# Grouped-query attention over a cached K and V: 256 rows of the output weights on four DMA engines, and four smaller edits

## The chip, the cores and the metric

The kernel runs on one core of a Trainium2 chip. The metric is the device time of one launch in microseconds, the median of several runs. Beside the times there is one profiled execution of the kernel, from which all rows below come.

## What is computed

Eight batches of four new tokens attend to 2,048 cached keys. There are 32 query heads and 8 K/V heads, so four query heads share a K/V head. All inputs are bf16.

```python
B, Sq, D = 8, 4, 512
Hq, Hkv, Sk, Dh = 32, 8, 2048, 128
q = (x @ wq).reshape(B, Sq, Hq, Dh).transpose(0, 2, 1, 3)
k = jnp.repeat(k_cache, rep, axis=1)          # rep = 4
v = jnp.repeat(v_cache, rep, axis=1)
scores = jnp.einsum("bhqd,bhkd->bhqk", q, k) * (Dh ** -0.5)
p = softmax(scores)
o = jnp.einsum("bhqk,bhkd->bhqd", p, v)
return o.transpose(0, 2, 1, 3).reshape(B, Sq, Hq * Dh) @ wo
```

K and V are 33.6 MB each, wq and wo 4.2 MB each: 75.5 MB are read once.

## The kernel before

**Units.** The work is cut into 16 units: four K/V heads of one batch each, `units[u] = (hq, b)`. One load of 2 MB brings a unit's K (`load_k`), another its V (`load_v`): 128 partitions, 16 KB contiguous in each. `kpool` and `vpool` hold three of each. All loads are issued by SP on one queue, in the order of the list `loads`: K two units ahead of V, and wo's first quarter between V13 and V14. `load_ready` issues as many as the buffers allow, once per unit; the other three quarters of wo are issued after the loop's unit 15. A load that has to wait holds up what stands behind it on SP. Each load also waits for the one issued eight loads before it, because eight completion semaphores are used in turn.

**One unit.** K arrives with keys in partitions. `transpose_part` (four parts to a unit) turns it on TensorE (PE), two bf16 as one fp32, into `kp` (pool `psum_k`, three banks), and VectorE (DVE) copies it to `kt`. `scores` multiplies with the block-diagonal queries `q_bd` into `s_ps`; ScalarE (ACT) takes EXP and leaves row sums in `l_sb`. `probs_to_keys` turns the result on PE into `pt` (pool `psum_t`, one bank), and ACT copies it in eight pieces to `probs`. `values` is 64 matmuls into `o_ps`, and `finish` writes `oT` and divides by the sums. `norms` makes the divisors in each unit: DVE's `by_gq`, a matmul with ones into `l_ps`, a reciprocal.

**Order.** The engines' orders are written out by hand (`manual_schedule`). Loop step n holds the turns of K of unit n, the scores of unit n - 1, and the values of unit n - 2.

**Output.** After eight units a half of the heads is complete. `to_tokens` turns it so that tokens lie in rows, `to_wo_rows` turns it again into `oP`, whose partitions match the layout of wo: eight rows of wo, 8 KB, in each partition. `project` multiplies with one quarter p of wo, 16 matmuls, accumulating into `out_ps`. The last quarter comes in two loads, six rows and two. After wo, four loads called `spare` of 5, 7, 1 and 3 rows of 64 bytes are issued, whose data nothing reads. ACT then copies `out_ps`, and two DMAs write the output.

Of the kernel before, what the change touches and what calls it, by code (L numbers as in the profile page):

```python
# [14 lines left out]
def kernel(  # L15
# [18 lines left out]
    G = 4  # L34
# [10 lines left out]
    KB, VB = 3, 3  # L45
    scale = float(Dh) ** -0.5
# [3 lines left out]
    assert Dh == 128 and C == 64 and J == 8 and HQ == 16 and NU == 16 and T == 32  # L50

# [6 lines left out]
    psum_k = ctx.enter_context(tc.tile_pool(name="psum_k", bufs=3, space=bass.MemoryType.PSUM))  # L58
# [3 lines left out]
    psum_l = ctx.enter_context(tc.tile_pool(name="psum_l", bufs=1, space=bass.MemoryType.PSUM))  # L62
# [6 lines left out]
    probs = [const.tile([128, C, G, HQ], BF16, name=f"probs{i}") for i in range(2)]  # L69
    ident = const.tile([128, 128], BF16, name="ident")  # L70
    ident4 = const.tile([128, 128], FP32, name="ident4")
    ones = const.tile([128, 128], FP32, name="ones")
    by_hq = const.tile([128, 2, HQ], FP32, name="by_hq")
    oT = [const.tile([128, HP, 2, B, Sq], BF16, name=f"oT{n}") for n in range(2)]
# [3 lines left out]
    spare = const.tile([16, 4, 32], BF16, name="spare")  # L78
# [5 lines left out]

    def load_k(u):
        hq, b = units[u]
        ks[u] = kpool.tile([128, C, Dh], BF16, tag="k_sb", name="k_sb")
        nc.sync.dma_start(
            ks[u][:, :, :],
            k_cache[b, G * hq : G * hq + G].rearrange("g (s c) d -> (g s) c d", c=C),  # L90
        )

    def load_v(u):
        hq, b = units[u]
        vs[u] = vpool.tile([128, C, Dh], BF16, tag="v_sb", name="v_sb")
        rows = v_cache[b, G * hq : G * hq + G].rearrange("g (s c) d -> (g s) c d", c=C)
        nc.sync.dma_start(vs[u][:, :, :], rows)

    def load_wo(p, r0, n):
        rows = wo[p * HP * 128 : (p + 1) * HP * 128, :].rearrange("(q r) j -> q r j", r=WR)  # L100
        nc.sync.dma_start(wo_sb[:, p, r0 : r0 + n, :], rows[:, r0 : r0 + n, :])  # L101

    load_k(0)
# [3 lines left out]
    for u in range(2, NU + 2):  # L107
        if u < NU:
            loads.append(("k", u))
        if u == NU:  # L110
            loads.append(("w", 0))
        loads.append(("v", u - 2))
    loads.reverse()

    def load_ready(nk, nv):

        while loads:
            kind, u = loads[-1]
            if kind == "w":
                load_wo(u, 0, WR)  # L120
            elif u >= (nk + KB if kind == "k" else nv + VB):
                return
            else:
                (load_k if kind == "k" else load_v)(u)
            loads.pop()
# [6 lines left out]
    nc.gpsimd.memset(probs[0][:, :, :, :], 0.0)  # L132
    nc.gpsimd.memset(probs[1][:, :, :, :], 0.0)  # L133
    nc.gpsimd.memset(ones[:, :], 1.0)
    nc.vector.tensor_reduce(
        out=by_hq[:, :, :],
        in_=ident4[:, :].rearrange("p (z c q) -> p z q c", z=2, q=HQ),
        axis=AX,
        op=ADD,
# [4 lines left out]
    def transpose_part(u, t):  # L144

        k4 = ks[u][:, :, :].rearrange("s c d -> s (c d)").bitcast(FP32)
        if t % 2 == 0:
            kt[(u, t // 2)] = ktpool.tile([128, 2 * J, 128, 2], BF16, tag="kt", name="kt")
        for half in range(2):
            j0 = t % 2 * J + half * J // 2  # L150
            kp = psum_k.tile([128, J // 2, 128], FP32, tag="k", name="kp")
            for j in range(J // 2):
                w = (t * J + half * J // 2 + j) * 128
                nc.tensor.transpose(kp[:, j, :], k4[:, w : w + 128], ident4[:, :])  # L154
            nc.vector.tensor_copy(  # L155
                out=kt[(u, t // 2)][:, j0 : j0 + J // 2, :, :].rearrange("k j s e -> k (j s e)"),
                in_=kp[:, :, :].rearrange("k j s -> k (j s)").bitcast(BF16),
            )
# [52 lines left out]
    l_sbs = {}  # L211

    def scores(u):

        hq, b = units[u]
        s_sbs[u] = small.tile([128, J, 2, S, 2], BF16, tag="s_sb", name="s_sb")
        l_sbs[u] = small.tile([128, 2], FP32, tag="l_sb", name="l_sb")
        for y in range(2):
            s_ps = psum_s.tile([128, 2 * J, S], FP32, tag="s", name="s_ps")
            for e in range(2):  # L220
                for m in range(4):
                    g, th = m // 2 * 2 + y, m % 2
                    nc.tensor.matmul(  # L223
                        s_ps[m * 32 : (m + 1) * 32, :, :],
                        lhsT=q_bd[:, hq, e, g, b, :, :],
                        rhs=kt[(u, th)][:, :, g * S : (g + 1) * S, e],
                        start=(e == 0),
                        stop=(e == 1),
                    )
            nc.scalar.activation(  # L230
                out=s_sbs[u][:, :, y, :, :].rearrange("r j s w -> r j w s"),
                in_=s_ps[:, :, :].rearrange("r (j w) s -> r j w s", w=2),
                func=EXP,
                accum_out=l_sbs[u][:, y : y + 1],
            )

    def probs_to_keys(u):
# [7 lines left out]
        pr = probs[u % 2][:, :, :, :].rearrange("s (x i k w) g q -> s x g i k w q", x=2, k=4, w=2)  # L245
        for x in range(2):
            for g in range(G):
                z, y = g // 2, g % 2
                nc.scalar.copy(  # L249
                    out=pr[g * S : (g + 1) * S, x, g, :, :, :, :],  # L250
                    in_=halves[(2 * x + y) * S : (2 * x + y + 1) * S, z, :, :, :, :],
                )

    r_sbs = {}

    def norms(u):
        by_gq = small.tile([128, 2, 2, HQ], FP32, tag="by_gq", name="by_gq")
        nc.vector.tensor_tensor(  # L258
            out=by_gq[:, :, :, :],
            in0=l_sbs[u][:, :].unsqueeze(1).unsqueeze(3).to_broadcast([128, 2, 2, HQ]),  # L260
            in1=by_hq[:, :, :].unsqueeze(2).to_broadcast([128, 2, 2, HQ]),
            op=MULT,
        )
        l_ps = psum_l.tile([128, NQ], FP32, tag="l", name="l_ps")
        nc.tensor.matmul(  # L265
            l_ps[:, :],
            lhsT=ones[:, :],
            rhs=by_gq[:, :, :, :].rearrange("k z y q -> k (z y q)"),
            start=True,
            stop=True,  # L270
        )
        r_sbs[u] = small.tile([128, NQ], FP32, tag="r_sb", name="r_sb")
        nc.vector.reciprocal(r_sbs[u][:, :], l_ps[:, :])  # L273
# [3 lines left out]
    def values(u, half):  # L277
        if half == 0:
            o_pss[u] = psum_o.tile([128, NQ], FP32, tag="o", name="o_ps")
        for i in range(half * C // 2, (half + 1) * C // 2):  # L280
# [4 lines left out]
                rhs=probs[u % 2][:, i, :, :].rearrange("s g q -> s (g q)"),  # L285
# [4 lines left out]
    def finish(u):  # L290
        hq, b = units[u]
        nc.vector.tensor_tensor(  # L292
            out=oT[hq][:, :, :, b, :].rearrange("d h p s -> d p h s"),
            in0=o_pss[u][:, :].rearrange("d (p h s) -> d p h s", p=2, h=HP),
            in1=r_sbs[u][:, :].rearrange("d (p h s) -> d p h s", p=2, h=HP),
            op=MULT,
        )

    def to_tokens(n):
        nat = psum_l.tile([2 * T, HP, 128], BF16, tag="l", name="nat")  # L300
        for h in range(HP):
            nc.tensor.transpose(
                nat[:, h, :], oT[n][:, h, :, :, :].rearrange("d p b s -> d (p b s)"), ident[:, :]
            )
        nc.vector.tensor_copy(out=nat_sb[:, :], in_=nat[:, :, :].rearrange("t h d -> t (h d)"))

    def to_wo_rows(n):
        perm = psum_l.tile([128, WR, 2, T], BF16, tag="l", name="perm")
        by_row = nat_sb[:, :].rearrange("t (q r) -> t r q", r=WR)
        for r in range(WR):  # L310
            nc.tensor.transpose(
                perm[:, r, :, :].rearrange("q p t -> q (p t)"), by_row[:, r, :], ident[: 2 * T, : 2 * T]
            )
        nc.vector.tensor_copy(out=oP[n][:, :, :, :], in_=perm[:, :, :, :])

    def project(p, r0, n):
        for r in range(r0, r0 + n):
            for half in range(2):
                nc.tensor.matmul(  # L319
                    out_ps[half * T : (half + 1) * T, :],  # L320
                    lhsT=oP[p // 2][:, r, p % 2, :],
                    rhs=wo_sb[:, p, r, half * DH : (half + 1) * DH],
                    start=(p == 0 and r == 0),
                    stop=(p == NP - 1 and r == WR - 1),
                )

    for n in range(1, NU + 2):
# [7 lines left out]
        if w >= 0:  # L335
            norms(w)
        if n < NU:
            transpose_part(n, 2)
        if n == NU - 1:
            probs_to_keys(n - 1)  # L340
        if n == NU + 1:
            out_ps = psum_s.tile([2 * T, DH], FP32, tag="s", name="out_ps")
            project(0, 0, WR)
# [16 lines left out]
        if n == NU - 1:  # L360
            assert not loads, loads
            for p, r0, k in [(1, 0, 8), (2, 0, 8), (3, 0, 6), (3, 6, 2)]:
                load_wo(p, r0, k)
            for i, k in enumerate([5, 7, 1, 3]):
                nc.sync.dma_start(spare[:k, i, :], x.flatten_outer_dims()[:k, :32])

    to_tokens(1)
    project(1, 0, WR)
    to_wo_rows(1)
    project(2, 0, WR)  # L370
    for r in range(0, WR, 2):
        project(3, r, 2)
# [34 lines left out]
```

## Time and profile before

| | |
|---|---|
| median of 3 runs | 187.62 us (187.45, 187.62, 190.75) |
| the profiled execution's own time | 187.35 us |
| its span | 185.6 us |
| PE, DVE, ACT busy | 74%, 56%, 55% of the span |
| HBM read | 75.53 MB, 407 GB/s over the span |
| packets of the load queue (q1) | 95.9% of 16 engines' span |
| granted TensorE clock, mean | 0.98 |

The span runs from the first to the last thing that the profiler records; 1.75 us of the execution's time lie around it. In groups of instructions a row reads: line, engine, operation, output<-input, count, then busy microseconds and mean nanoseconds of one, then the engine's idle time before them and what ended it. A queue row gives packets, megabytes and the time that the packets took as a share of the 16 DMA engines' time. A wait row gives microseconds in total, times, and the longest. `q8 instruction` and `q14 instruction` are transfers that bring the engines their own instructions.

### The profile page before, as it was taken

What the parts mean: (1) busy time and instruction counts of PE and PEld (TensorE: products, weight loads), DVE (VectorE), ACT (ScalarE), POOL (GpSimd) and SP (SyncE); (2) the same over time, 40 slices, a digit from 0 to 9 for tenths busy, and PEclk for the clock granted to TensorE, in tenths of its full rate; (3) what the DMA queues carried; (4) which work ended last, traced back from release to release, by engine and by line L of the source; (5) the groups of instructions that cost most, each with busy time, mean ns of one, the idle gap of its engine ahead of it and who ended that gap; (6) DMA issues with size and microseconds to landing.
All of it is one profiled execution on the core that took longest, in us unless ns stands there. A gap on an engine that the chain in (4) does not pass through costs nothing.

```text
span 185.6 us, 4659 instructions
## 1 busy us (share of the span) xinstructions
PE 137.2 (74%) x2036; PEld 113.4 (61%) x2036; DVE 103.6 (56%) x189; ACT 102.2 (55%) x200; POOL 8.2 (4%) x11
## 2 busy tenths in 40 slices
PE   0092869797978777777777869579777777795872
PEld 0192347595866665757575849377666757585651
DVE  4074188777765747475665756466747475661220
ACT  2000153969576666574839292927566574878700
POOL 8900000000000000000000000000000000000000
PEclk9999589999999999999999999999999999999999
DMA  6998999999999999999999999999999999999970
GB/s 187 484 438 378 434 424 431 434 420 431 438 422 431 422 438 410 441 431 424 434 427 431 434 417 431 441 413 438 424 434 434 417 443 420 417 443 411 417 297 8
DMA packets 5668, 75.86 MB, mean 409 GB/s; under 512 B 688, under 2 KB 784, under 8 KB 1040
## 3 DMA queue, kind: packets, MB, share of 16 engines
q1 hardware_dynamic: 5600, 75.55, 95.9%
q8 instruction: 16, 0.26, 0.5%
q14 instruction: 4, 0.03, 0.0%
q10 hardware_dynamic: 48, 0.02, 0.0%
HBM read 75.53 MB, written 0.03 MB: 407 GB/s over the span
## 4 chain that ended last, share of the span: by engine, by line
DMA 68%; PE 22%; DVE 4%; issue 1%; ACT 1%; SPq 1%
DMA k_sb<-in_k_cache_dram 46%; DMA wo_sb<-in_wo_dram 13%; PE kp L154 12%; DMA x_sb<-in_x_dram 9%; DVE kt L155 3%; PE s_ps L223 3%; PE o_ps L282 3%; PE psq L177 2%; PE l_ps L265 1%; ACT q_bd L202 1%; PE out_ps L319 1%; SPq L101 0%; PE pt L242 0%; DVE by_gq L258 0%; DVE q_bd L202 0%
## 5 line engine op out<-in xcount | busy, mean ns | idle before, releaser
L155 DVE COPY kt<-kp 128x1024 bf16<-128x1024 bf16 x128 | 82.0, 683 | 42.7 <-PE kp L154 42.7
L249 ACT COPY probs<-pt 32x512 bf16<-32x512 bf16 x128 | 73.7, 576 | 49.5 <-PE pt L242 46.7
L154 PE MATMUL kp<-ident,k_sb 128*128 128x128 f32 x512 | 70.6, 284 | 20.2 <-DMA k_sb<-in_k_cache_dram 11.2
L154 PEld LDWEIGHTS kp<-ident,k_sb 128*128 128x128 f32 x512 | 58.3, 147 | 28.8 <-DVE oT L292 9.7
L282 PE MATMUL o_ps<-probs,v_sb 128*128 128x64 bf16 x1024 | 34.8, 194 | 0.2 <-DMA v_sb<-in_v_cache_dram 0.2
L282 PEld LDWEIGHTS <-v_sb 128*128 128x128 bf16 x1024 | 33.9, 98 | 0.8 <-DMA v_sb<-in_v_cache_dram 0.5
L230 ACT ACTIVATE s_sb<-s_ps 128x512 bf16<-128x512 f32 x32 | 22.6, 734 | 1.3 <-PE s_ps L223 0.9
L265 PE MATMUL l_ps<-by_gq,ones 128*128 128x64 f32 x32 | 6.9, 298 | 15.6 <-DVE by_gq L258 15.6
L223 PE MATMUL s_ps<-kt,q_bd 128*32 128x512 bf16 x256 | 17.5, 390 | 0.0
L265 PEld LDWEIGHTS l_ps<-by_gq,ones 128*128 128x128 f32 x32 | 4.8, 188 | 19.5 <-DVE by_gq L258 17.7
L273 DVE RECIPROCAL r_sb<-l_ps 128x64 f32<-128x64 f32 x16 | 8.9, 558 | 9.1 <-PE l_ps L265 9.1
L186 ACT ACTIVATE q_nat<-psq 128x512 bf16<-128x512 f32 x2 | 1.2, 597 | 20.4 <-PE psq L177 20.4
L242 PE MATMUL pt<-ident,s_sb 128*128 128x128 f32 x64 | 9.7, 274 | 2.1 <-ACT s_sb L230 2.1
L292 DVE TENSOR_TENSOR oT<-o_ps,r_sb 128x64 bf16<-128x64 f32 x16 | 3.6, 225 | 13.6 <-PE o_ps L282 13.5
L223 PEld LDWEIGHTS <-q_bd 128*32 128x32 bf16 x256 | 5.6, 94 | 6.1 <-issue 2.5
L242 PEld LDWEIGHTS pt<-ident,s_sb 128*128 128x128 f32 x64 | 7.4, 141 | 2.3 <-ACT s_sb L230 2.3
L230 ACT ACTIVATION_READ_ACCUMULATOR s_sb<-s_ps 128x1 f32 x32 | 6.0, 188 | 0.0
L319 PE MATMUL out_ps<-wo_sb,oP 128*32 128x256 bf16 x64 | 4.2, 273 | 1.1 <-DMA wo_sb<-in_wo_dram 0.6
L374 ACT CAST out_sb<-out_ps 64x256 bf16<-64x256 f32 x1 | 0.4, 365 | 6.9 <-PE out_ps L319 6.9
L319 PEld LDWEIGHTS <-oP 128*32 128x32 bf16 x64 | 3.0, 96 | 1.7 <-issue 0.7
L177 PE MATMUL psq<-wq_sb,xT_sb 128*32 128x512 bf16 x32 | 3.6, 631 | 0.3 <-DVE xT_sb L170 0.3
L133 POOL MEMSET probs<- 128x4096 bf16 x1 | 3.5, 3512 | 0.0
(27 smaller groups left out, 29.9 us busy)
## 6 DMA issues: line engine op xcount, KB each, us to landing
k_sb<-in_k_cache_dram SPq DMA_DIRECT2D x16, 2048.0 KB, 21.6
v_sb<-in_v_cache_dram SPq DMA_DIRECT2D x16, 2048.0 KB, 25.1
wq_sb<-in_wq_dram SPq DMA_DIRECT2D x1, 4096.0 KB
wo_sb<-in_wo_dram SPq DMA_DIRECT2D x3, 1024.0 KB, 20.9
wo_sb<-in_wo_dram SPq DMA_DIRECT2D x1, 768.0 KB, 23.2
wo_sb<-in_wo_dram SPq DMA_DIRECT2D x1, 256.0 KB, 23.4
x_sb<-in_x_dram SPq DMA_DIRECT2D x1, 32.0 KB
spare<-in_x_dram SPq DMA_DIRECT2D x1, 0.3 KB
```

The source lines that it names most:

```text
L154: nc.tensor.transpose(kp[:, j, :], k4[:, w : w + 128], ident4[:, :])
L155: nc.vector.tensor_copy(out=kt[(u, t // 2)][:, j0 : j0 + J // 2, :, :].rearrange("k j s e -> k (j s e)"), in_=kp[:, :, :].rearrange("k j s ...
L177: nc.tensor.matmul(psq[g * T : (g + 1) * T, :], lhsT=xT_sb[:, r, :], rhs=wq_sb[:, r, c0 : c0 + rep * Dh], start=(r == 0), stop=(r == R - 1),)
L223: nc.tensor.matmul(s_ps[m * 32 : (m + 1) * 32, :, :], lhsT=q_bd[:, hq, e, g, b, :, :], rhs=kt[(u, th)][:, :, g * S : (g + 1) * S, e], star ...
L230: nc.scalar.activation(out=s_sbs[u][:, :, y, :, :].rearrange("r j s w -> r j w s"), in_=s_ps[:, :, :].rearrange("r (j w) s -> r j w s", w= ...
L242: nc.tensor.transpose(pt[:, i, :], s4[:, i * 128 : (i + 1) * 128], ident4[:, :])
L249: nc.scalar.copy(out=pr[g * S : (g + 1) * S, x, g, :, :, :, :], in_=halves[(2 * x + y) * S : (2 * x + y + 1) * S, z, :, :, :, :],)
L265: nc.tensor.matmul(l_ps[:, :], lhsT=ones[:, :], rhs=by_gq[:, :, :, :].rearrange("k z y q -> k (z y q)"), start=True, stop=True,)
L273: nc.vector.reciprocal(r_sbs[u][:, :], l_ps[:, :])
L282: nc.tensor.matmul(o_pss[u][:, :], lhsT=vs[u][:, 2 * (th * 2 * J + 2 * (2 * j + x) + w) + c, :], rhs=probs[u % 2][:, i, :, :].rearrange("s ...
L292: nc.vector.tensor_tensor(out=oT[hq][:, :, :, b, :].rearrange("d h p s -> d p h s"), in0=o_pss[u][:, :].rearrange("d (p h s) -> d p h s", ...
L319: nc.tensor.matmul(out_ps[half * T : (half + 1) * T, :], lhsT=oP[p // 2][:, r, p % 2, :], rhs=wo_sb[:, p, r, half * DH : (half + 1) * DH], ...
```

## The change

- **wo.** The first 128 rows of each of wo's first two quarters (256 rows, 256 KB) go to a tile `wo_e` of their own, in partitions 0 to 15 and 32 to 47, by eight loads (`load_wo_e`) of four partitions with 8 KB each. They are issued after V2 to V9, one each. Their counterpart of the attention output is `oE`. In the first two quarters of `wo_sb` a partition then holds seven rows instead of eight.
- **Order of loads.** All of the rest of wo is issued after V15, in ten loads (`WO_PARTS`). K15 and V15 are loaded in two halves. The `spare` loads are gone.
- **Sums.** `norms` is gone. `finish` only copies; `to_tokens` makes all the divisors of a half at once (`by_tok` on GpSimd, two matmuls into `l_ps`, one reciprocal) and divides while it copies `nat` out, with tokens in rows. `oT` and `nat` are fp32.
- **K turns.** `kp` covers two banks, in two buffers, and DVE copies 2,048 bf16 values a time instead of 1,024.
- **Probabilities.** Two of the eight copies of a unit go to DVE (four in the last unit), and `probs` is four tiles of half a unit. `l_ps` and `perm` are taken from `psum_t`, `nat` from `psum_k`.
- The last unit but one turns its probabilities before the third part of K's turns. The projection stands behind the loop.

```diff
+    WO_PARTS = [(p, r, n) for p in (0, 1) for r, n in ((0, 4), (4, 3))]
+    WO_PARTS += [(2, 0, 4), (2, 4, 4)] + [(3, r, 2) for r in range(0, WR, 2)]
+    NE, WM = 48, 7
...
-    psum_k = ctx.enter_context(tc.tile_pool(name="psum_k", bufs=3, space=bass.MemoryType.PSUM))
+    psum_k = ctx.enter_context(tc.tile_pool(name="psum_k", bufs=2, space=bass.MemoryType.PSUM))
...
+    def load_kv(to, cache, u, parts=1):
+        hq, b = units[u]
+        rows = cache[b, G * hq : G * hq + G].rearrange("g (s c) d -> (g s) c d", c=C)
+        for i in range(parts):
+            cs = slice(i * C // parts, (i + 1) * C // parts)
+            nc.sync.dma_start(to[:, cs, :], rows[:, cs, :])
...
+        load_kv(ks[u], k_cache, u, 2 if u == NU - 1 else 1)
...
+    def load_wo_e(i):
+        p0, k0 = i // 4 * 32 + i % 4, i // 4 * HP * 128
+        rows = wo[k0 : k0 + 16 * WR, :].rearrange("(q r) j -> q r j", r=WR)
+        nc.sync.dma_start(wo_e[p0 : p0 + 13 : 4, :, :], rows[i % 4 : i % 4 + 13 : 4, :, :])
+
     def load_wo(p, r0, n):
-        rows = wo[p * HP * 128 : (p + 1) * HP * 128, :].rearrange("(q r) j -> q r j", r=WR)
+        w, k0 = (WM, p * HP * 128 + 16 * WR) if p < 2 else (WR, p * HP * 128)
+        rows = wo[k0 : (p + 1) * HP * 128, :].rearrange("(q r) j -> q r j", r=w)
         nc.sync.dma_start(wo_sb[:, p, r0 : r0 + n, :], rows[:, r0 : r0 + n, :])
 
+    nc.gpsimd.memset(wo_e[:, :, :], 0.0)
     load_k(0)
...
-        if u == NU:
-            loads.append(("w", 0))
         loads.append(("v", u - 2))
+        if 4 <= u < 12:
+            loads.append(("e", u - 4))
...
-        for half in range(2):
-            ...
+        kp = psum_k.tile([128, J, 128], FP32, tag="k", name="kp")
+        for j in range(J):
+            w = (t * J + j) * 128
+            nc.tensor.transpose(kp[:, j, :], k4[:, w : w + 128], ident4[:, :])
+        nc.vector.tensor_copy(
...
+                on_dve = x == 1 if u == NU - 1 else g == 0
+                (nc.vector.tensor_copy if on_dve else nc.scalar.copy)(
...
-    def norms(u):
...
     def to_tokens(n):
+        by_tok = small.tile([128, 2, 2, B, Sq], FP32, tag="by_tok", name="by_tok")
+        for y in range(2):
+            nc.gpsimd.tensor_tensor(
+                out=by_tok[:, y, :, :, :],
...
+        l_ps = psum_t.tile([2 * T, 2, rep], FP32, tag="t", name="l_ps")
...
+        nc.vector.reciprocal(r_sb[:, :], l_ps[:, :, :].rearrange("t y h -> t (y h)"))
+        nat = psum_k.tile([2 * T, HP, 128], FP32, tag="k", name="nat")
+        for h0 in range(0, HP, 4):
...
+            nc.vector.tensor_tensor(
+                out=nat_sb[:, h0 * 128 : (h0 + 4) * 128].rearrange("t (h d) -> t h d", h=4),
+                in0=nat[:, h0 : h0 + 4, :],
+                in1=r_sb[:, h0 : h0 + 4].unsqueeze(2).to_broadcast([2 * T, 4, 128]),
+                op=MULT,
+            )
...
-            for p, r0, k in [(1, 0, 8), (2, 0, 8), (3, 0, 6), (3, 6, 2)]:
+            for p, r0, k in WO_PARTS:
                 load_wo(p, r0, k)
-            for i, k in enumerate([5, 7, 1, 3]):
-                nc.sync.dma_start(spare[:k, i, :], x.flatten_outer_dims()[:k, :32])
...
+    out_ps = psum_s.tile([2 * T, DH], FP32, tag="s", name="out_ps")
     to_tokens(1)
-    project(1, 0, WR)
-    to_wo_rows(1)
-    project(2, 0, WR)
-    for r in range(0, WR, 2):
-        project(3, r, 2)
+    for r in range(WR):
+        project(wo_e[:, r], oE[:, r, :], first=r == 0)
+    for p in range(NP):
+        if p == 2:
+            to_wo_rows(1)
+        for r in range(WM if p < 2 else WR):
+            project(wo_sb[:, p, r], oP[p // 2][:, r, p % 2, :], last=p == NP - 1 and r == WR - 1)
```

## The prediction

> **What bounds the kernel now.** I read the page's slices and queue rows first, then the chain that ended last, SP's waits, and last the tail in half-microsecond windows.
>
> ```profile
> DMA  6998999999999999999999999999999999999970
> ...
> q1 hardware_dynamic: 5600, 75.55, 95.9%
> q8 instruction: 16, 0.26, 0.5%
> q14 instruction: 4, 0.03, 0.0%
> ...
> DMA 68%; PE 22%; DVE 4%; issue 1%; ACT 1%; SPq 1%
> ...
> k_sb<-in_k_cache_dram SPq DMA_DIRECT2D x16, 2048.0 KB, 21.6
> ```
>
> From the second slice to the 38th the 16 DMA engines are as good as full. 75.55 MB pass, and neither kernel moves fewer. The chain is transfers for 68% of the span. A K load lands 21.6 us after its issue, though its own packets take 8 x 0.607 = 4.86 us on each engine: 16.7 us of other work is queued ahead of it.
>
> ```profile
> SPq L88 <- PE kp L154: 94.6, 13, 8.2
> ...
> SPq L365 <- DMA v_sb<-in_v_cache_dram: 12.6, 3, 4.6
> ```
>
> SP issues a K load when PE has turned the old one. Its long waits cost nothing while that queue is full, and PE waits for K too:
>
> ```profile
> PE kp L154 <- DMA k_sb<-in_k_cache_dram: 11.2, 11, 1.9
> ```
>
> So compute has slack in every unit. What can move the end is how the queue drains. In these windows the last two columns are the share of 16 engines busy and GB/s:
>
> ```profile
> 177.50:178.00 0.50, 0.50 (x12) 0.33 (x8) 0.37 (x1) 0.00 (x0) 0.00 (x0) 1.00 1.01 414
> 178.00:178.50 0.50, 0.50 (x11) 0.44 (x8) 0.00 (x0) 0.00 (x0) 0.00 (x0) 1.00 0.78 316
> ...
> 179.50:180.00 0.50, 0.50 (x14) 0.46 (x10) 0.00 (x0) 0.00 (x0) 0.00 (x0) 1.00 0.61 230
> ...
> 180.50:181.00 0.50, 0.11 (x3) 0.11 (x4) 0.00 (x0) 0.00 (x0) 0.00 (x0) 1.00 0.30 115
> 181.00:181.50 0.50, 0.50 (x12) 0.50 (x10) 0.00 (x0) 0.00 (x0) 0.00 (x0) 1.00 0.02 8
> ```
>
> The engines do not stop together: from 178 to 181.2 us fewer and fewer work. The first is done at 177.84, the last at 181.18.
>
> **Why they differ.** No view prints single packets, but the trace holds their start, length and size, and they can be followed: a 16 KB packet is followed on its engine by the next 607 ns later, and each load gives each engine eight packets and a 4-byte completion. Followed so, all 16 engines carry the same 4.72 MB. An engine falls behind by 1.42 us when a 16 KB instruction packet (q8) passes through it, by 0.55 to 0.88 us at an 8 KB one (q14), and by up to 1.1 us at the start. The q8 packets come after every 256 or so PE instructions and go round eight engines; seven of these had two each and end at 180.49 to 181.18, the eighth had one in time and ends at 179.75. The ACT stream's two q14 packets (60.6 and 150.9 us, 63 and 191 ACT instructions in) hit one engine, which ends at 179.50; the two I take for DVE's (52.2 and 159.4 us) another, which ends at 179.87. The other six end at 177.84 to 178.76.
>
> Which engines get the new four-row loads can be read from the old `spare` loads of 5, 7, 1 and 3 rows. Their 64-byte packets stand at the ends of seven engines, in numbers 4, 3, 3, 2, 2, 1, 1: the sets are nested. These engines end at 178.11 (4); 178.45 and 179.50 (3); 177.87 and 179.87 (2); 180.49 and 180.68 (1). A four-row load goes to the first three and one of the two with 2. All are engines without q8 packets, but the three include ACT's. [...]
>
> **The change on the queue.** Packet intervals in the trace: 8 KB 0.305 us, 6 KB 0.230, 2 KB 0.080, completion 0.006. 4 and 3 KB packets are not there; between the 2 and 6 KB rows they are 0.155 and 0.117.
> - wo before, per engine: 24 x 0.305 + 8 x 0.230 + 8 x 0.080 + 5 x 0.006 = 9.83 us.
> - wo after on all 16: 16 x 0.155 + 16 x 0.117 (p = 0, 1), 16 x 0.155 (p = 2), 32 x 0.080 (p = 3), ten completions: 9.45 us.
> - K15 and V15 in halves: 32 x 0.305 for 16 x 0.607, two completions more: +0.06.
> - So every engine saves 0.32 us, and the four pay 8 x (0.305 + 0.006) = 2.49 for `wo_e`: net +2.17.
>
> Counted in the two built programs, PE has 4,090 instructions for 4,096, so q8 stays. ACT has 203 for 238, still past 191: its second packet moves to unit 15's EXP near 168 us, before the end. DVE has 174 for 215: its second packet goes. With the old start offsets:
> - the seven with q8: latest 181.18 - 0.32 = 180.86;
> - the clean ones of the four: at most 178.45 + 2.17 = 180.62;
> - ACT's: 179.50 + 2.17 = **181.67**;
> - DVE's, if it is the fourth: 179.87 - 0.84 + 2.17 = 181.20.
>
> The last byte moves from 181.18 to 181.67: **+0.49 us**. Bounds: 180.86 (-0.32), if ACT's second packet or start offset falls away, and 182.04 (+0.86), if DVE's is among the four and keeps both packets.
>
> [...]
>
> **The tail.** A landing reached PE 0.35 us after the slowest engine's last packet (`wo_sb` part 3a: 180.54, PE at 180.89).
>
> ```profile
> 180.89 1.05 PE L319 MATMUL out_ps<-wo_sb,oP 128*32 128x256 bf16 x16 [0.56 <-DMA wo_sb<-in_wo_dram]
> ...
> 181.97 0.36 ACT L374 CAST out_sb<-out_ps 64x256 bf16<-64x256 f32 x1 [6.92 <-PE out_ps L319]
> ```
>
> The last part was visible at 181.53, while these 16 ran, so the cast came 0.79 us after the last byte. After the change four matmuls wait for the last byte: 0.35 + 0.273 + 3 x 0.052 + 0.03 = 0.81. No gain (+0.02).
>
> **What is hidden, and by what.**
> - PE behind V15: its second half reaches PE near 172.6 (181.67 less 9.45 us of wo, and 0.35). Then 32 values 1.03, `finish` 0.35, eight fp32 turns 1.06, 44 `project` matmuls 2.9, `to_wo_rows` 1.2, p = 2 1.05, twelve of p = 3 0.8: 8.4 us, done near 181.0, while the last byte reaches PE at 182.0. Cover 1.0 us; what is beyond falls on the end. The sums (POOL's two small operations after EXP near 169, two matmuls) run ahead of the turns: 3 us of cover.
> - In the loop DVE loses 128 x 0.683 and 16 x (0.22 + 0.558), and gains 64 x 1.29 (two old copies end to end took that; between 0.68 and 1.37) and 34 probability copies at 0.43 to 0.69 (nearest: 64x1024 `nat_sb` 0.68, 128x512 `oP` 0.43; I take ACT's 0.576): -99.9 + 102.2, about level. PE loses the 15.6 us it waited for `by_gq`. Hidden behind the K waits.
> - `l_ps` and `perm` now share `psum_t` with `pt`: in units 8 and 9 PE stands behind ACT's six copies, 3.5 us each time, and the next K turns stand behind PE. Against 16.7 us queued: nothing.
> - SP issues eleven more DMAs at 0.3 to 0.45 us. An added load waits for the DMA eight before it, a transfer older than the one K waits for. Behind it stand K and V loads; same cover.
> - POOL clears `wo_e` ahead of the identities: 3.5 us (`probs`, 128x4096), identities at 5.2; K0 lets PE start at 8.8. Without that cover PE starts late, yet x lands only at 18.1.
>
> **Sum.** The profiled execution took 187.35 with a span of 185.6; the median is 187.62 and the lower two runs 187.45 and 187.62, so I add to 187.5: 187.5 + 0.49 + 0.02 = **188.0 us**.
>
> **Rivals.**
> 1. *The balance works* (187.2): ACT's engine starts early or loses a packet, and the q8 engines decide at 180.86. For: start offsets differ by up to 1.1 us, and nothing says they repeat. Against: ACT still passes instruction 191. 0.29.
> 2. *The fourth engine is DVE's, with both packets* (188.4): 182.04. Against: 174 instructions. 0.12.
> 3. *The four-row loads do not spread* but sit on one engine: 32 packets x 0.311 = 9.95, so 178.11 - 0.32 + 9.95 = 187.74, 6.6 us late: 194. For: the one-row load did so. Against: the nested spares. It passes 2% from 23 packets on one engine (3.4 us of lead and 3.75). 0.03.
> 4. *`psum_t` starves the queue*: it needs more than 16.7 us of delay at units 8 and 9 and costs what is beyond, so 21 us would make it 192. For: two new waits on one bank. Against: 3.5 us each. 0.02.
> 5. *Over 2% faster* needs 3.75 us, but the mean engine ends at 179.65, so perfect levelling gives 1.5. 0.02.
>
> The forecast has 0.52. The range takes in the bounds, -0.32 and +0.86, and some 0.4 us of run scatter and start offsets on each side: 186.8 to 188.9. Two per cent (3.75 us) is about what a measurement of this kernel can tell from no change; faster, same, slower: 0.02, 0.93, 0.05.
>
> **What would show it.** Right: the drain is shorter but ends later, at 181.4 to 182; K and V loads still land 20 us after issue; three q14 packets instead of four, sixteen q8; the last matmul group is four and waits for `wo_sb`; no `l_ps` rows in the loop. Wrong: gaps in the DMA row before 170 us, a last group waiting for DVE or ACT, or a queue end below 181.

## Result, and the profile after

The changed kernel takes 204.8 us (median of 4 runs, 204.07 to 206.99) against 187.7 us for the kernel before on the same chip: a ratio of 1.094 [1.083, 1.104]. The forecast was 188.0, in a range that ended at 188.9. The profiled execution took 204.72 us with a span of 202.9 (before: 187.35 and 185.6). Some executions of a kernel come out 1.5% or more above its fastest (before: 190.75 for 187.45 us), and the ratios leave these out, so that medians and ratios need not rank alike.

Of the page of the changed kernel, the slices (5.07 us each), the queue rows and the chain:

```profile
PEclk9999769999999999999999975785699999699769
DMA  6999999999999999999999999999999999991000
GB/s 213 446 452 400 423 436 429 423 433 429 423 439 420 431 425 433 423 436 426 429 426 436 426 426 442 420 426 439 426 352 446 365 354 323 409 382 71 3 3 6
...
q1 hardware_dynamic: 6640, 75.55, 89.1%
q8 instruction: 16, 0.26, 0.5%
q14 instruction: 4, 0.03, 0.0%
...
DMA 33%; PE 31%; ACT 19%; DVE 11%; issue 3%; SPq 0%; ACTq 0%; DVEq 0%
```

Three things differ from before. The transfers end three slices before the program does, so something else sets the end: their share of the chain has gone from 68% to 33%, and ACT and DVE, 1% and 4% before, now hold 30%. The clock row, all nines in the second half before, has a hole from slice 24 to 29 (117 to 147 us) and others near the end. And the moved bytes thin out from slice 30 on (147 us): the queue, never short of work before, is now fed late (SP's longest wait for PE's K turns, 8.2 us before, is 14.7). The packet kinds are as before; there are still four q14 packets.

PE's waits show new rows (the last line here is SP's):

```profile
PE l_ps L309 <- ACT probs L270: 5.0, 1, 5.0
PE perm L338 <- ACT probs L270: 4.9, 1, 4.9
...
PE o_ps L282 <- DVE oT L292: 3.9, 1, 3.9
...
SPq L99 <- PE kp L176: 77.2, 13, 14.7
```

The first two are the two uses of `psum_t` for which the prediction had 3.5 us each "against 16.7 us queued: nothing". The timeline shows the first of them (start, duration, work, and in brackets the wait before):

```profile
115.13 1.23 DVE L177 COPY kt<-kp 128x2048 bf16<-128x2048 bf16 x1 [1.33 <-PE kp L176]
...
116.27 1.37 DVE L270 COPY probs<-pt 32x512 bf16<-32x512 bf16 x2
...
117.75 3.58 ACT L270 COPY probs<-pt 32x512 bf16<-32x512 bf16 x6 [4.94 <-DVE probs L270]
...
121.42 0.56 PE L309 MATMUL l_ps<-by_h,by_tok 128*64 128x4 f32 x4 [4.97 <-ACT probs L270]
```

`pt` is complete at 115.5. DVE takes its two copies out of it first, but stands behind a `kt` copy until 116.27; ACT takes its six only then, until 121.33. For all that time `pt` holds the only buffer of `psum_t`, and PE, which would have gone on with the next unit's K, stands at `l_ps`. In windows around this wait (busy time of PE, weight loads, DVE, ACT, POOL; then granted clock, DMA share, GB/s):

```profile
113.00:117.00 4.00, 3.38 (x76) 3.25 (x76) 2.65 (x4) 0.00 (x0) 0.00 (x0) 1.00 1.01 430
117.00:121.00 4.00, 0.00 (x0) 0.00 (x0) 0.86 (x2) 3.13 (x6) 0.00 (x0) 0.72 0.99 422
121.00:125.00 4.00, 2.80 (x14) 2.18 (x15) 1.03 (x3) 0.33 (x1) 0.00 (x0) 0.50 1.03 442
125.00:129.00 4.00, 4.00 (x28) 2.29 (x27) 1.76 (x2) 1.38 (x3) 0.00 (x0) 0.50 0.99 422
```

The transfers go on at full rate in all four rows. But the clock falls to 0.50 and stays there for 7.6 us after PE has work again (121.4 to 129.0). Eight K turns that took 1.07 us before the wait, at 114.02, take 1.92 behind it, at 124.61. So one wait of 5 us costs PE more than 5 us. When PE begins to turn each unit's K shows the sum (us from the start of the span; "step" is the time from one unit to the next):

| unit | 10 | 11 | 12 | 13 | 14 | 15 |
|---|---|---|---|---|---|---|
| before | 107.3 | 118.4 | 128.1 | 137.8 | 147.5 | 157.2 |
| after | 108.3 | 124.6 | 140.5 | 150.1 | 158.1 | 165.8 |
| after is late by | 1.0 | 6.2 | 12.4 | 12.3 | 10.6 | 8.6 |
| step after | | 16.3 | 15.9 | 9.6 | 8.0 | 7.7 |

Before, the queue sets a step of 9.7 us. PE without hindrance needs some 7.7, so it wins back 2 us a unit. Three units are left after the second wait, and K15 starts 8.6 us late.

The rest is lost behind it. From the start of K15 to ACT's copy of `out_ps` before takes 24.7 us (157.2 to 181.97), after 34.2 (165.8 to 200.08). The tail of the changed kernel:

```profile
185.28 0.57 ACT L270 COPY probs<-pt 32x512 bf16<-32x512 bf16 x1 [0.76 <-DVE probs L270]
185.89 0.70 DVE L270 COPY probs<-pt 32x512 bf16<-32x512 bf16 x1 [0.64 <-ACT probs L270]
...
186.99 3.57 PE L282 MATMUL o_ps<-probs,v_sb 128*128 128x64 bf16 x64 [3.87 <-DVE oT L292]
...
193.81 3.17 PE L355 MATMUL out_ps<-wo_sb,oP 128*32 128x256 bf16 x28
...
200.08 0.37 ACT L406 CAST out_sb<-out_ps 64x256 bf16<-64x256 f32 x1 [14.22 <-PE out_ps L355]
```

PE has nothing to do until the last unit's eight copies are made by ACT and DVE in turn, and until DVE, behind its share of them, has copied unit 14's result to `oT`, which is the wait that ends last. Then it runs at half clock in two stretches (187.0 to 190.4 and 193.8 to 197.3): 64 `values` matmuls in 3.57 us, which took 2.03 for unit 14, and 28 projections in 3.17. Before, the first quarter of the projection stood in exactly this gap.

### The profile page after: what moved, and what is told of

It reads as the page before. It is cut to its first block, busy times and chain, and to the rows that moved or that the text cites. A ratio compares the mean times of both kernels' runs of the same rounds, so it can differ in the third digit from the quotient of the medians.

```text
span 202.9 us, 4597 instructions
## 1 busy us (share of the span) xinstructions
PE 146.6 (72%) x2031; PEld 118.7 (58%) x2031; DVE 112.9 (56%) x134; ACT 83.0 (41%) x166; POOL 13.0 (6%) x18
## 4 chain that ended last, share of the span: by engine, by line
DMA 33%; PE 31%; ACT 19%; DVE 11%; issue 3%; SPq 0%; ACTq 0%; DVEq 0%
DMA v_sb<-in_v_cache_dram 25%; ACT probs L270 14%; PE kp L176 11%; DMA x_sb<-in_x_dram 8%; PE o_ps L282 8%; DVE probs L270 5%; DVE kt L177 4%; ACT s_sb L250 4%; PE out_ps L355 3%; PE s_ps L243 3%; PE pt L262 2%; PE nat L321 2%; PE psq L199 2%; PE perm L338 1%; DVE nat_sb L326 1%
## 5 line engine op out<-in xcount | busy, mean ns | idle before, releaser
L177 DVE COPY kt<-kp 128x2048 bf16<-128x2048 bf16 x64 | 76.9, 1222 | 47.0 <-PE kp L176 46.7
L176 PE MATMUL kp<-ident,k_sb 128*128 128x128 f32 x512 | 72.6, 295 | 19.2 <-DMA k_sb<-in_k_cache_dram 15.9
L270 ACT COPY probs<-pt 32x512 bf16<-32x512 bf16 x94 | 54.2, 577 | 65.6 <-DVE probs L270 57.8
L176 PEld LDWEIGHTS kp<-ident,k_sb 128*128 128x128 f32 x512 | 61.5, 152 | 28.5 <-issue 10.1
L282 PE MATMUL o_ps<-probs,v_sb 128*128 128x64 bf16 x1024 | 37.2, 198 | 10.7 <-DMA v_sb<-in_v_cache_dram 4.7
L270 DVE COPY probs<-pt 32x512 bf16<-32x512 bf16 x34 | 23.1, 679 | 8.2 <-ACT probs L270 5.4
L243 PE MATMUL s_ps<-kt,q_bd 128*32 128x512 bf16 x256 | 20.1, 431 | 0.1
L151 POOL MEMSET probs<- 128x2048 bf16 x4 | 7.0, 1805 | 0.0
L292 DVE COPY oT<-o_ps 128x64 f32<-128x64 f32 x16 | 3.6, 224 | 4.2 <-PE o_ps L282 3.8
L338 PE MATMUL perm<-ident,nat_sb 64*128 64x64 bf16 (+1 forms) x23 | 1.8, 236 | 5.7 <-ACT probs L270 4.9
```

The lines of the kernel that those rows point to most:

```text
L151: nc.gpsimd.memset(probs[i][:, :, :, :], 0.0)
L177: nc.vector.tensor_copy(out=kt[(u, t // 2)][:, t % 2 * J : (t % 2 + 1) * J, :, :].rearrange("k j s e -> k (j s e)"), in_=kp[:, :, :].rearr ...
L243: nc.tensor.matmul(s_ps[m * 32 : (m + 1) * 32, :, :], lhsT=q_bd[:, hq, e, g, b, :, :], rhs=kt[(u, th)][:, :, g * S : (g + 1) * S, e], star ...
L270: (nc.vector.tensor_copy if on_dve else nc.scalar.copy)(out=pr[g * S : (g + 1) * S, g, :, :, :, :], in_=halves[(2 * x + y) * S : (2 * x + ...
L282: nc.tensor.matmul(o_pss[u][:, :], lhsT=vs[u][:, 2 * (th * 2 * J + 2 * (2 * j + x) + w) + c, :], rhs=probs[u % 2 * 2 + x][:, i % 32, :, :] ...
L338: nc.tensor.transpose(perm[: by_row.shape[2], r, :, :].rearrange("q p t -> q (p t)"), by_row[:, r, :], ident[: 2 * T, : 2 * T],)
```

## The experiments

Kernels of one section ran on one chip with the kernel before, whose medians were 187.63, 189.13 and 187.94 us in the three. The changed kernel itself ("after") was measured on another chip. Line numbers differ a little between kernels.

**1. One suspect at a time.** Theory A: the shared bank makes most of the 17 us. Theory B: the split of the copies over ACT and DVE, with its alternation, does. Four kernels: each undone alone, both undone, and the bank shared in the kernel before.

```diff
# e1: bank of their own
-        l_ps = psum_t.tile([2 * T, 2, rep], FP32, tag="t", name="l_ps")
+        l_ps = psum_k.tile([2 * T, 2, rep], FP32, tag="k", name="l_ps")
-            perm = psum_t.tile([128, WR, 2, T], BF16, tag="t", name="perm")
+            perm = psum_k.tile([128, WR, 2, T], BF16, tag="k", name="perm")
# e2: ACT makes all copies
-                on_dve = x == 1 if u == NU - 1 else g == 0
+                on_dve = False
# e3: both of these
# e4: the kernel BEFORE, with
-        nat = psum_l.tile([2 * T, HP, 128], BF16, tag="l", name="nat")
+        nat = psum_t.tile([2 * T, HP, 128], BF16, tag="t", name="nat")
-        perm = psum_l.tile([128, WR, 2, T], BF16, tag="l", name="perm")
+        perm = psum_t.tile([128, WR, 2, T], BF16, tag="t", name="perm")
```

> The changed kernel (204.8 us) with l_ps and perm taken from psum_k instead of psum_t. Theory A (the end is late because PE stands behind the copies of pt in units 8 and 9, 5.0 + 4.9 us, with the clock at 0.5 after each, and because the tail behind K15 is longer by itself): the two waits go, K15's turns start near 158 instead of 165.8, but the tail keeps the serial copies of unit 15 on two engines, so 194 to 198 us. Rival B (only the shared bank costs): 187 to 189. Rival C (the queue ran dry and the bank does not matter): 203 to 205.

> The changed kernel with all copies of pt on ACT, l_ps and perm still in psum_t. Theory A: the waits of l_ps and perm shrink by about 1 us each only, so most of the lag stays, and the last unit's values no longer wait for finish behind DVE's copies (3 us): 198 to 202 us. Rival D (passing the bank between DVE and ACT is what costs, in the loop and at the end): below 193.

> The changed kernel with both edits: l_ps and perm from psum_k, all copies of pt on ACT. Theory A: the lag and the serial copies go, 188 to 191 us. The forecast on record for the queue alone says 188.0. If something else costs (two-bank turns of K, sums on tokens), it stays above 192.

> The kernel before with nat and perm taken from psum_t instead of psum_l, nothing else. Theory A: PE waits 3.5 to 5 us for ACT's copies after units 8 and 9, the clock halves, and as a step can be made up by only some 1.1 us a unit (8.6 against 9.7), 3 to 9 us remain at the end: 191 to 197. Rival (the queue of 16.7 us hides it, as the prediction on record said): 187 to 188.5.

| | split copies | ACT alone |
|---|---|---|
| shared bank | 204.8 (after) | 195.92, ratio 1.044 [1.034, 1.054] (e2) |
| own bank | 196.21, ratio 1.042 [1.034, 1.050] (e1) | 193.07, ratio 1.025 [1.016, 1.034] (e3) |

e1 falls where A had it, e2 below what was expected (198 to 202). Neither theory alone is right. In these medians the two cost more together than singly: the bank 2.9 us where ACT copies alone, 8.6 with the split; the split 3.1 and 8.9. But the intervals of e2 and e3 overlap, and K15 starts 5.9 us later in e2 than in e3 (161.8 for 155.9), so 2.9 is not safe as the price of the bank: e4 below and e10 in part 3 give 5.8 and 5.7. What the traces show is that the split lengthens the time for which the bank is held, and so the waits (4.0 and 4.0 us in e2, 5.0 and 4.9 after) and the stretches at half clock behind them (6.8 and 6.8 us in e2, 10.2 and 10.2 after). Both undone still leave 5.4 us over the kernel before, more than A and B had (the expectation was 188 to 191). So there was a third cause.

e4 came out at 193.41, ratio 1.035 [1.026, 1.044]: the same bank, shared in the kernel before, costs 5.8 us by itself. Its waits, and the window after the first:

```profile
PE perm L311 <- ACT probs L249: 4.0, 1, 4.0
PE nat L302 <- ACT probs L249: 4.0, 1, 4.0
```

```profile
121.00:125.00 4.00, 4.00 (x30) 2.12 (x28) 1.90 (x4) 1.57 (x4) 0.00 (x0) 0.61 1.03 442
```

In the kernel before the clock is 1.00 in this window. Eight K turns take 1.71 us behind e4's wait, and the 16 `scores` matmuls after them 1.90; before, both took 1.06. K15 starts at 163.3 for 157.2, yet the last byte of the queue comes at 181.18, to the hundredth where it came before. The queue did not starve; PE came late, and there was too little time left to make it up.

**2. The tail.** In e3 K15 starts on time (155.9) and the last byte comes at 181.62, but the copy of `out_ps` only at 188.96: 33.1 us from K15 on, nearly the 34.2 of after. Its gap and its windows:

```profile
175.03 2.54 PE L282 MATMUL o_ps<-probs,v_sb 128*128 128x64 bf16 x64 [2.46 <-ACT probs L270]
...
175.00:180.00 5.00, 4.19 (x73) 3.56 (x73) 1.11 (x3) 0.58 (x1) 0.00 (x0) 0.63 0.91 359
180.00:185.00 5.00, 5.00 (x44) 3.12 (x45) 0.68 (x1) 0.00 (x0) 0.00 (x0) 0.50 0.11 41
```

From 180 to 185 us PE is full and at half clock. Two theories: PE idles 2.46 us for the copies, work is missing from that gap, and what follows has to be made up (idle time); or the clock, lowered by that gap, is the cost. e5 fills the gap with projections that are ready, as the kernel before did; e6 moves unit 14's turns back as well; e8 fills it with 16 turns of the identity that nothing reads, so PE does more, nothing is earlier, and only the clock can gain. e7 is the kernel before with the 256 rows on four engines, alone.

```diff
# e5: e3, and ahead of the last unit's values (these projections are then not made behind the loop)
+        if n == NU + 1:
+            out_ps = psum_s.tile([2 * T, DH], FP32, tag="s", name="out_ps")
+            for r in range(WR):
+                project(wo_e[:, r], oE[:, r, :], first=r == 0)
+            for r in range(WM):
+                project(wo_sb[:, 0, r], oP[0][:, r, 0, :])
# e6: e5, and
-        if n == NU - 1:
-            probs_to_keys(n - 1)
         if n < NU:
             transpose_part(n, 2)
+        if n == NU - 1:
+            probs_to_keys(n - 1)
# e8: e3, and ahead of the last unit's values
+        if n == NU + 1:
+            kp = psum_k.tile([128, J, 128], FP32, tag="k", name="kp")
+            for j in range(2 * J):
+                nc.tensor.transpose(kp[:, j % J, :], ident4[:, :], ident4[:, :])
# e7: the kernel BEFORE, with load_wo_e, oE, wo_e and WM = 7 as in the change
```

> e3 (193.1 us) with the projections of wo_e and of p = 0 moved ahead of the last unit's values, where PE waits 2.5 us for ACT's copies, as the kernel before had its first quarter there. Theory A (the rest of the loss is PE's idle wait and the half clock that follows it over the tail): PE loses some 1.6 us of work after the wait and the clock holds: 188.5 to 190. Rival E (the queue's end, 181.6 in e3, already sets the time): 192 to 193.5.

> e5 with probs_to_keys of unit 14 behind the third part of K15's turns again, as in the kernel before. Theory A: PE no longer stands 2.5 us before EXP of unit 14 and the clock does not fall at 160 to 165, so unit 15 comes some 2 us earlier; with the queue then deciding, 187.5 to 188.5 (the forecast for the queue alone was 188.0). Rival: no change against e5.

> The kernel before with the 256 rows of wo on four engines and nothing else of the change (wo's first two quarters with seven rows a partition, eight small loads, wo_e and oE). Queue sum: all engines save 0.6 us, the four pay 2.5: ACT's engine ends at 179.50 + 1.88 = 181.4 for 181.18, so 187.7 to 188.2. [...] Rival (the levelling works): 187.0 to 187.3.

> e3 with 16 throwaway turns of the identity on PE while it waits for ACT's copies of the last unit; all other work where it was. Theory A's part on the clock: the 44 projections and the turns behind them run at the full clock, 189 to 190.5 for 193.1. If only the idle time itself counts and not the clock, nothing is gained: 192.5 to 193.5.

- e5: 188.33, ratio 1.001 [0.997, 1.005], a little better than expected. No difference from the kernel before.
- e8: 189.58, ratio 1.004 [0.999, 1.008], as expected. Its filled gap and its windows:

```profile
170.94 1.95 PE L380 MATMUL kp<-ident 128*128 128x128 f32 x16
173.56 2.03 PE L282 MATMUL o_ps<-probs,v_sb 128*128 128x64 bf16 x64 [0.67 <-ACT probs L270]
...
175.00:180.00 5.00, 4.22 (x70) 3.25 (x68) 1.79 (x4) 0.00 (x0) 0.00 (x0) 1.00 0.92 364
180.00:185.00 5.00, 3.08 (x50) 2.33 (x46) 0.42 (x1) 0.36 (x1) 0.00 (x0) 1.00 0.12 44
```

Work that does nothing, put into the gap, keeps the clock at 1.00, and the copy of `out_ps` comes at 183.64 for 188.96. Not all of this is due to the filling. The profiled execution of e8 lacks a stretch at half clock that e3 and e5 have near 162 to 166 us, and so its unit 14 starts `values` 1.5 us earlier (169.07 for 170.55 and 170.54), ahead of the gap. From the end of unit 14's `values` to the copy e3 takes 16.4 us, e8 12.5 and e5 11.2. So the clock is worth 3.8 us, the larger part, and the work that is missing from the gap another 1.3. The medians of e8 and e5 differ by as much, but their intervals overlap.

- e6: 190.79, of four runs between 188.19 and 193.2, without an interval: inconclusive; no gain is seen. In its profiled execution the half clock near 162 us is gone, as expected, and unit 14's `values` start at 169.09; but e8's start at 169.07 without this edit, and another stretch, from 175.6 to 179.0, takes the gain back.
- e7: 189.08, ratio 0.998 [0.993, 1.003]. The 256 rows on four engines make no difference that can be measured, and the interval is too wide to confirm or exclude the 0.5 us that the sum put on them.

**3. Back on the mended tail, and a better version.** e9 and e10 put the split and the shared bank back into e5, one each. e11 reorders ACT's copies so that those which the first `values` need come first, with only `wo_e`'s projections in the gap; e12 is e11 with the 256 rows in two loads of 16 partitions. That these go over all 16 engines is an estimate from the `spare` loads, whose 7 rows stood on seven engines.

```diff
# e9: e5, and
-                on_dve = False
+                on_dve = x == 1 if u == NU - 1 else g == 0
# e10: e5, with l_ps and perm from psum_t again
# e11: e5, and
-        for g in range(G):
-            for x in range(2):
+        for x in range(2):
+            for g in range(G):
...
-            for r in range(WM):
-                project(wo_sb[:, 0, r], oP[0][:, r, 0, :])
# e12: e11, and
-        p0, k0 = i // 4 * 32 + i % 4, i // 4 * HP * 128
-        nc.sync.dma_start(wo_e[p0 : p0 + 13 : 4, :, :], rows[i % 4 : i % 4 + 13 : 4, :, :])
+        p0, k0 = i // 4 * 32, i // 4 * HP * 128
+        if i % 4 == 0:
+            nc.sync.dma_start(wo_e[p0 : p0 + 16, :, :], rows)
```

> e5 (188.3 us) with the copies of pt split over DVE and ACT again as in the change (two of eight on DVE, alternating four and four in the last unit). Theory A: in the loop the longer bank time (5.8 for 5.0 us) hides behind the wait for K; in the last unit the copies take 5.3 for 4.8 us in turns, and finish of unit 14 stands behind them on DVE, so the last values start 1 to 2 us later: 189 to 190.5. Rival (the split costs only together with the shared bank): 188.0 to 188.6.

> e5 with l_ps and perm in psum_t again. Theory A: PE waits 4 us twice, the clock halves twice, and some 6 us of lag remain at K15's turns (161.8 in e2 against 155.9), which all reach the end: 191 to 194. Rival (with the tail mended the lag is made up): 188 to 189.5.

> e5 with the copies of pt in the order of the kernel before (all of x = 0 first) and only wo_e projected ahead of the last values. The last values can start after four copies instead of seven and no longer wait for p = 0 of wo (174.97 in e5), so PE should be ready before the last byte of wo: the queue decides, last byte at 181.7 to 181.9, cast 0.8 us later: 187.0 to 187.8.

> e11 with the same 256 rows loaded by two DMAs of 16 partitions (all 16 engines) instead of eight of four (four engines). Queue sum: the four engines save 8 x 0.311 and pay 2 x 0.311, the others pay 0.62: last byte 181.2 to 181.7 instead of 181.8, so equal within 0.5 us: 186.8 to 187.8. If the four engines were the limit it gains up to 0.6, if the rows level the queue it loses up to 0.6.

- e10: 194.07, ratio 1.032 [1.027, 1.036], at the upper end of what was expected. The shared bank costs 5.7 us on this tail, as it cost 5.8 in e4. K15 starts at 161.0 for e5's 155.9.
- e9: four runs, two at 189.1 and two near 193, no interval. What the split costs alone is left open; the intervals of e1 and e3, whose medians are 3.1 us apart, touch.
- e11: 188.39, ratio 0.998 [0.995, 1.002], where 187.0 to 187.8 was expected. Its lowest runs, 186.85 to 186.97, are under the lowest of the kernel before (187.39), but the interval holds 1. A gain is not shown. The last byte was expected at 181.7 to 181.9; in the profiled execution, which at 189.75 us lies above the median, it comes at 182.98.
- e12: 190.74, ratio 1.014 [1.009, 1.019], expected equal to e11. The queue shows it: the last byte comes at 184.04. First e12, then e5, whose rows come by four-partition loads:

```profile
50.00:52.00 2.00, 2.00 (x33) 1.24 (x29) 1.14 (x3) 1.93 (x4) 0.00 (x0) 1.00 1.31 418
52.00:54.00 2.00, 2.00 (x20) 1.73 (x16) 1.18 (x2) 1.93 (x4) 0.00 (x0) 1.00 0.65 213
```

```profile
50.00:52.00 2.00, 2.00 (x37) 1.39 (x33) 1.14 (x3) 1.90 (x5) 0.00 (x0) 1.00 0.96 410
52.00:54.00 2.00, 2.00 (x24) 1.75 (x17) 1.17 (x2) 1.93 (x4) 0.00 (x0) 1.00 1.06 442
```

A packet that started in the first row of e12 and took longer counts there, so 1.31 and 0.65 belong together: 418 and 213 GB/s moved with the engines never idle. Nearly fifty packets of 16 KB around the two loads took 1.0 to 1.5 us for 0.61, and those of the loads up to 0.81 for 0.31.

## Why the prediction was wrong, step by step

**The step that failed** is the line on `psum_t` under "What is hidden", and rival 4 with it. The place was right: the bank, and units 8 and 9. Three things in its price were not.

- *The cover.* It set the waits against the 16.7 us of transfers queued ahead of a K load. In e4, where nothing else is edited, that depth protects the queue from a late PE: the last byte stays at 181.18 us. It does not protect the end, which comes 5.8 us later: PE's own work is behind by what it waited, and a lag is hidden only as far as PE makes it up before the end. The numbers for that were in the trace of before: a wait for K of under 2 us in a unit ("11.2, 11, 1.9") is all that PE has to spare there, and the two waits fall with few units left.
- *The size.* 3.5 us were six of ACT's copies. The bank is held from 115.5 to 121.3: DVE's `kt` copy comes ahead of its two copies, and those ahead of ACT's six. 5.0 and 4.9 were measured.
- *The clock.* After such a wait PE runs at half clock: from 118.7 to 129 us here, 10.2 us. The prediction had no such term, though the page of before has slices at 0.5 and 0.8 early on. The length of a gap alone does not tell what the clock does: the waits of 4.0 us in e2 were followed by 6.8 us at 0.50, the gap of 2.46 us in e3 by 10 us; one of 2.13 us at 167.4 in the kernel before had no such effect, and neither had one of 3.47 us at 158.9 in e9.

**The tail** failed next, "8.4 us ... Cover 1.0 us". It let `values` of unit 15 start when V15 lands, near 172.6. They also need the unit's probabilities: in e3 they start at 175.03 and end at 177.57, and with the clock kept up (e5) end at 177.44, where the sum had 173.6. So the 1.0 us of cover was gone even at full clock (the copy of `out_ps` comes 1.88 us after the last byte in e5, for the 0.81 of the sum), and at half clock 33.1 us from K15 on for 27.8. What the prediction did not cost at all is the gap that a removal opens: it counted the 44 projections behind V15 (2.9 us), but not that `project(0, 0, WR)` no longer stands ahead of the last `values`. In the kernel before PE's waits there are 2.13, 0.45 and 0.22 us, with the clock at 1.00.

**How 17 us come together.** K15 starts 8.6 us late (the bank, held longer by the split), and from there on it takes 9.5 us longer (clock, copies in turn, no filling): 18.1 at the copy of `out_ps` (17.4 in the span: what comes after the copy is 0.7 us shorter). With the bank apart and ACT alone 5.4 us remain, and filling the gap takes these away.

**What held.**
- The sum of the queue: the last byte was put at 181.67. Where PE keeps up it is measured at 181.62 (e3), 181.88 (e5), 181.82 (e8); in e2 and e10, whose PE is late but not late enough to starve it, at 181.57 and 181.56. That it is so close may be in part luck: the sum had one instruction packet too few (below), and which engine ended last was not followed in the new traces. In the changed kernel itself the last byte comes at 185.2, since late K turns made late K loads.
- The four-row loads spread, and cost the packets' time: in the trace of after the four packets of each of the first two loads start within 0.24 us, all 32 took 0.309 us each, and while the eight ran, a step was 10.0 us for 9.7 to 9.8. Rival 3 did not occur.
- DVE about level: 64 `kt` copies took 76.9 us and 34 probability copies 23.1, together 100.0 for the 102.2 of the sum.
- PE gains by losing `norms`: a step without hindrance takes 7.1 to 7.7 us (e10, e2, after) for 8.5 to 8.6 (e4). Behind a queue that gives a unit every 9.7 us this is worth nothing until there is a lag to make up.

**What did not show:** three q14 packets were forecast and four came (after at 70.5, 71.8, 175.5 and 182.6 us), so the count of DVE's instructions was no guide. The last group waiting for `wo_sb`, and a drain that decides, were on the list of what would show the prediction right; the rows show neither.

**Not tried alone:** K15 and V15 in halves, wo behind them, the divisors by tokens, the K turns over two banks. All are in e5, which with them is level with the kernel before; whether one gains what another loses is open.

## What to carry to other kernels

The depth of the transfer queue hid a late engine from the queue, not from the end of the program (in e4 the last byte did not move, and 5.8 us were lost): price a new wait by what the waiting engine can make up in the units that are left, here 2 us each. When a buffer's tag is shared, follow who empties it and what stands ahead of them on their own engines; here a split over two engines held a bank longer than one engine did (PE waited 5.0 us for 4.0). Before a piece of work is moved out of a gap on PE, look what clock the rest will run at: 16 useless turns in a gap of 2.5 us were worth about 4 us (12.5 us for 16.4 from unit 14's `values` to the copy, e8 and e3).

## What was not expected of the hardware

- The stretches at half clock measured here last 3.41 us, twice that or three times that: 10.24 us behind each bank wait after, 6.8 behind each in e2 and e10, 10.2 in e3's tail (176.3 to 186.6), 3.41 twice in the tail after (187.0 to 190.4 and 193.8 to 197.3). PE was busy through most of e3's stretch (5.00 of the 5.00 us from 180 to 185); why it lasted three times as long as those two is open.
- The same wait need not have the same effect. PE stands 2.50 us before 161.5 in e3, e5 and e8 alike; in e3 and e5 3.4 us at half clock follow, in e8 none. No run shows what decides.
- Eight loads of four partitions cost the queue nothing beyond their bytes that the trace of after shows (0.309 us for each packet, as for 8 KB in the trace of before); two of 16 partitions, with the same bytes, slowed their neighbours in e12 (1.0 to 1.5 us for 0.61). The page of e12 has two dips, at slices 12 and 20 to 21. They lack 91, 98 and 39 GB/s against 430; times 4.74 us that is 1.08 MB, or 2.5 us of the queue; the two loads land at 55.5 and 95.9 us, within these slices:

```profile
GB/s 187 477 443 394 422 418 436 439 436 418 422 339 430 425 422 425 436 429 430 332 391 432 422 439 429 422 436 425 439 418 432 432 410 436 429 422 410 412 205 9
```

Why these loads slow their neighbours no run shows.
